# Two 64-row remainders of neighbouring batches put through the second feed-forward product as one block of 128 rows

## The chip, the cores and the metric

The kernel runs on one core of a Trainium2 chip. The metric is the time of one execution on the device in microseconds (us). The engines are TensorE (PE in the profile; PEld are its weight loads), VectorE (DVE), ScalarE (ACT), GpSimd (POOL) and SyncE (SP), which issues all transfers here.

## The reference

Eight batches of 576 tokens go through two parts. The first is attention with eight heads of 64 channels, in which each row of the scores keeps its 32 largest entries:

```python
scores = scale * np.matmul(q, k.transpose(0, 1, 3, 2))
kth = np.partition(scores, -top_k, axis=-1)[..., -top_k:-top_k + 1]
scores = np.where(scores >= kth, scores, -1000000000.0)
attn = softmax(scores); attn_out = np.matmul(attn, v)
```

The second is a feed-forward part on x (576 x 512 for a batch), with a convolution of three taps along the tokens as its gate:

```python
h = np.maximum(x @ w_in, 0.0)                        # 576 x 1024
conv_out = sum(conv_w[k] * hp[:, k:k + S, :] for k in range(3))
return (h * sigmoid(conv_out)) @ w_out               # 576 x 512
```

## The kernel before

Attention is cut into 288 tiles of 128 query rows: 8 batches x 4 pairs of heads x 9 tiles. `iteration(it)` writes one step of a pipeline in which each of five or six tiles is at another stage: PE makes the scores of tile it+3, ACT copies those of tile it+2 out of PSUM, DVE searches the candidates of tiles it and it-1 (L235, L255, L257), ACT and POOL mark and flip the entries of tile it-2 (L268, L273), ACT takes the exponential of tile it-3 (L280), DVE selects the threshold (`select`, L287) and weighs the exponentials of tile it-4 (L293), and PE transposes those of tile it-5 (L306) and multiplies them with v (L337, L340). Up to the last tile the order of the instructions on PE, ACT, DVE and POOL is that in which `iteration` writes them (a manual schedule). Behind it, in the tail, the framework's scheduler orders them.

The feed-forward part of a batch is laid between these steps. `ffn` (L567) cuts the 576 rows into part 0 (rows 0 to 255) and part 1 (rows 256 to 575). `Expand` (eight units for each part, one for each 128 columns of h) makes h with 12 matmuls (L404), relu on ACT (L418), the taps on POOL (in the tail on DVE, L457), tanh on ACT (L465) and the gate on DVE (L473); the result stays in the buffer `g0` or `g1`, of which each part has one. `Contract` makes the second product. Its `split` casts a piece of the gated h on ACT into a high part (L514), and POOL (DVE in the tail) subtracts to get the low part (L517). Then three matmuls for each 128 columns of h (high x high, high x low, low x high) add up in one PSUM bank, with the rows as the stationary operand and 512 columns of w_out as the moving one (L536). A block of 128 rows is two units of 12 matmuls (`half` 0 and 1, four of the eight column blocks each), since one slot of the `split` buffer holds 8 x 64 columns of high and of low part. The last 64 rows of a batch are one unit of 24 matmuls: eight column blocks with 64 rows each fill the same slot. `emit` copies the bank out (L552) and SP writes it to memory (L553).

A budget sets how much of this work an iteration gets: `run_units` spends a credit of 1.42 for each iteration (`FEED`), in units of planned cost, first on `Expand`, then on `Contract`. An `Expand` starts at most every second iteration (`PACE`), and not before every block of the same part of earlier batches has left `unready`, that is, has been read out of `g`. One `split` is written in an iteration, as long as fewer than three slots are taken (`SPB`). In the tail all of them are freer: four slots, several expands in flight, and both a PSUM bank of their own and one that the attention no longer needs (`mc`, `weights_ps`).

Of the kernel before, what the change touches and what calls it, by code (L numbers as in the profile page):

```python
# [63 lines left out]
def attend_and_feed(ctx: ExitStack, tc: tile.TileContext, q, k, v, weights, out, shared, finish=None):  # L64
# [313 lines left out]
    class Expand:  # L378
# [103 lines left out]
        def gated(self):  # L482
            self.gs["done"] = self.gs.get("done", 0) + 1
            state.flying -= 1

    class Contract:
        def __init__(self, b, part, s0, half, gs, box):
            self.b, self.part, self.s0, self.gs, self.box = b, part, s0, gs, box
            self.m = min(P, ROWS[part][1] - ROWS[part][0] - s0)
            nf = NFT * TAIL // self.m  # L490
            self.fs = range(half * nf, half * nf + nf)
            self.first, self.final, self.ready = half == 0, self.fs[-1] == NFT - 1, False
            self.count = nf
            self.cost = nf * 3 * (DM / 2400 + 0.012)

        def split(self):
            if not parts:
                parts.append(moe.tile([P, SPB, 2, NFT * TAIL], F32R, name="split"))
            late = state.it > NT + 4
            if late and len(parts) == 1:  # L500
                for pool, name, n, size in ((att, "e2", EBUFS, 2 * S), (att, "pT", 2, 2 * MAIN)):
                    for _ in range(n):
                        t = pool.tile([P, size], F32R, name=name, bufs=n)
                        extra.append(t[:, 0:2 * NFT * TAIL].rearrange("p (i c) -> p i c", i=2))
                parts.extend(extra)
            both = extra[state.split % len(extra)] if late else parts[0][:, state.split % SPB]
            self.hi, self.lo = (both[:, i].rearrange("p (f m) -> p f m", m=self.m) for i in range(2))
            self.late = late
            c0 = self.gs["at"] + self.s0
            src = self.gs["g"][:, self.fs[0]:self.fs[-1] + 1, c0:c0 + self.m]  # L510
            state.split += 1
            state.splits += 0 if late else 1
            state.late_splits += 1 if late else 0
            nc.scalar.copy(out=self.hi, in_=src)  # L514

            def rest(engine):
                engine.tensor_tensor(self.lo, src, f32(self.hi), ALU.subtract)  # L517
                self.ready = True
                unready.remove(self)

            if state.it > NT + 4:
                rest(nc.vector)
            else:
                pool_tasks.append((state.it + 1, 1.3, lambda: rest(nc.gpsimd)))
# [16 lines left out]
        def emit(self):  # L541
            m, mm = self.m, self.box.mm
            r = ROWS[self.part][0] + self.s0
            if state.it > NT + 4:
                if not outs_late:
                    t = const.tile([P, XBUFS * (S + 16)], F32, name="rows")
                    outs_late.extend(t[:, i * DM:(i + 1) * DM] for i in range(XBUFS * (S + 16) // DM))
                o = outs_late[0]
                outs_late.append(outs_late.pop(0))
            else:  # L550
                o = moe.tile([P, DM], F32, name="o", bufs=OB)
            nc.scalar.copy(out=o[0:m], in_=mm[0:m])  # L552
            nc.sync.dma_start(out=out[self.b, r:r + m, :], in_=o[0:m])  # L553

    parts, extra, outs_late, unready = [], [], [], []

    def split_next():
        if not unready or blocks or fetched or cut or acted or dved:
# [7 lines left out]
    def ffn(b, part):  # L566
# [2 lines left out]
        n = ROWS[part][1] - ROWS[part][0]  # L569
        for s0 in range(0, n, P):  # L570
            box = Box()
            units = [Contract(b, part, s0, half, gs, box) for half in range(1 if n - s0 == TAIL else 2)]
            contracts.extend(units)
            unready.extend(units)

# [365 lines left out]
```

## Time and profile before

| what | value |
|---|---|
| median of 3 runs | 1166.35 us (1164.91 to 1168.83) |
| profiled execution | 1168.88 us |
| its span (first to last instruction) | 1167.0 us |
| PE busy, PEld busy | 1056.8 us (91%), 775.1 us (66%) |
| DVE busy | 1066.8 us (91%) |
| ACT busy | 997.6 us (85%) |
| POOL busy | 896.1 us (77%) |
| matmuls of the second product (L536) | 960 |

The span has a beginning of some 200 us in which the weights are converted and no feed-forward work runs, a main part in which attention and feed-forward work share the engines, and from about 1076 us on the tail, in which only feed-forward work of the last two batches is left.

### The profile page before, as it was taken

The page shows a single profiled execution, that of the slowest core. Times are in us where ns is not written, and L with a number is a line of the kernel's source. Part 1 is how long each engine was busy: PE and PEld are TensorE (multiplying, and loading weights), DVE is VectorE, ACT ScalarE, POOL GpSimd, SP SyncE. Part 2 cuts the span into 40 slices and gives each one's busy share as a digit, 9 for nine tenths or more (in the row PEclk, how much of TensorE's full clock was granted, in tenths as well). Part 3 has the DMA queues.
Part 4 walks back from the last instruction along what each step waited for, and adds up shares of the span by engine and source line. Part 5 has one row for each costly group of instructions (what it writes and reads, how often), then busy time and mean ns, then how long its engine had stood idle before and what let it go on. Part 6 is the DMA issues. An engine that isn't in the chain of part 4 may idle for free.

```text
span 1167.0 us, 27441 instructions
## 1 busy us (share of the span) xinstructions
PE 1056.8 (91%) x8066; PEld 775.1 (66%) x8066; DVE 1066.8 (91%) x5832; ACT 997.6 (85%) x2335; POOL 896.1 (77%) x1072
## 2 busy tenths in 40 slices
PE   3665676888999999999999999999999999999996
PEld 1343344566767777776677777777777777777985
DVE  7999989999999999999999999999999999998550
ACT  5776778899999999999999999999999999998341
POOL 6778864789979888878879897888879887889100
PEclk9867659999999999999999999999999999999999
DMA  6220111101111111111111111111111111000001
GB/s 239 78 80 29 45 43 37 52 21 37 50 54 55 54 50 55 55 63 46 59 54 34 38 45 63 56 55 48 56 54 55 55 48 51 30 28 19 27 26 41
DMA packets 51695, 60.76 MB, mean 52 GB/s; under 512 B 9776, under 2 KB 30544, under 8 KB 51536
## 3 DMA queue, kind: packets, MB, share of 16 engines
q1 hardware_dynamic: 51536, 58.91, 15.8%
q8 instruction: 66, 1.08, 0.4%
q14 instruction: 93, 0.76, 0.2%
HBM read 49.31 MB, written 9.58 MB: 50 GB/s over the span
## 4 chain that ended last, share of the span: by engine, by line
PE 47%; DVE 42%; ACT 9%; issue 1%; DMA 0%; SPq 0%; POOL 0%; ACTq 0%; POOLq 0%
DVE cand L235 12%; PE mc L536 12%; DVE e L293 9%; PE me L404 8%; PE s_ps L337 6%; DVE z L283 6%; PE pt L306 6%; PE s_ps L219 5%; DVE cand L257 3%; DVE scratch L161 2%; ACT weights_ps L280 2%; PE s_ps L222 2%; DVE rows L255 2%; DVE hot L287 2%; PE weights_ps L536 2%; PE s_ps L214 2%
## 5 line engine op out<-in xcount | busy, mean ns | idle before, releaser
L273 POOL TENSOR_TENSOR z<-rows,side 128x579 f32<-128x579 f32 x288 | 347.9, 1208 | 148.6 <-ACT side L268 121.9
L235 DVE MAX8 cand<-rows 128x8 f32<-128x82 f32 (+1 forms) x2016 | 451.5, 238 | 0.1
L280 ACT ACTIVATE weights_ps<-rows,z 128x576 f32<-128x576 f32 x288 | 219.7, 763 | 41.4 <-DVE e L293 31.5
L293 DVE SCALAR_TENSOR_TENSOR e<-rows,kth,weights_ps 128x576 f32<-128x576 f32 x288 | 230.3, 800 | 0.3
L268 ACT ACTIVATE side<-rows 128x576 bf16<-128x576 f32 x288 | 223.9, 777 | 0.7 <-DVE rows L255 0.5
L404 PE MATMUL me<-x_hi,wi 128*128 128x322 f32 (+1 forms) x928 | 220.8, 310 | 1.2 <-ACT g L418 1.2
L228 ACT COPY rows<-s_ps 128x576 f32<-128x576 f32 x288 | 183.2, 636 | 38.8 <-PE s_ps L340 25.4
L283 DVE MAX8 z<-z 128x8 f32<-128x576 f32 x288 | 213.8, 742 | 0.0
L536 PE MATMUL mc<-wo,split 128*128 128x512 f32 (+1 forms) x756 | 205.1, 404 | 0.0
L219 PE MATMUL s_ps<-k,q 64*128 64x512 f32 x512 | 154.3, 680 | 51.2 <-ACT xt L348 36.7
L306 PE MATMUL pt<-ident,e 128*128 128x128 f32 x1152 | 191.7, 291 | 9.0 <-DVE e L293 9.0
L337 PE MATMUL s_ps<-pT,vn 128*64 128x128 f32 (+1 forms) x2560 | 171.2, 279 | 17.1 <-ACT rows L228 16.9
L337 PEld LDWEIGHTS s_ps<-pT,vn 128*64 128x64 f32 x2560 | 134.3, 143 | 54.0 <-ACT rows L228 25.7
L404 PEld LDWEIGHTS me<-x_hi,wi 128*128 128x128 f32 x928 | 157.5, 189 | 2.3 <-ACT g L418 1.9
L306 PEld LDWEIGHTS pt<-ident,e 128*128 128x128 f32 x1152 | 135.3, 148 | 35.3 <-issue 19.6
L311 ACT COPY pT<-pt 128x512 f32<-128x512 f32 x256 | 151.8, 593 | 3.8 <-PE pt L306 3.5
L536 PEld LDWEIGHTS mc<-wo,split 128*128 128x128 f32 (+1 forms) x756 | 126.5, 179 | 26.5 <-ACT o L552 0.2
L404 PE MATMUL me<-x_lo,wi 128*128 128x258 f32 (+1 forms) x464 | 138.8, 299 | 0.0
L437 POOL TENSOR_SCALAR t<-g,cr 128x256 f32<-128x256 f32 (+1 forms) x222 | 113.5, 511 | 0.0
L222 PEld LDWEIGHTS s_ps<-k,q 128*128 128x128 f32 x256 | 40.9, 201 | 104.9 <-issue 104.9
L255 DVE MAX8 rows<-cand 128x8 f32<-128x21 f32 x576 | 109.1, 189 | 0.0
L219 PEld LDWEIGHTS s_ps<-k,q 64*128 64x128 f32 x512 | 40.4, 193 | 83.8 <-ACT xt L348 47.5
(120 smaller groups left out, 1872.4 us busy)
## 6 DMA issues: line engine op xcount, KB each, us to landing
k<-in_k_dram SPq DMA_DIRECT2D x32, 352.0 KB
q<-in_q_dram SPq DMA_DIRECT2D x32, 288.0 KB
vn<-in_v_main_dram SPq DMA_DIRECT2D x32, 256.0 KB
rb<-row SPq DMA_DIRECT2D x64, 128.0 KB
out_dram<-o SPq DMA_DIRECT2D x24, 256.0 KB
raw<-in_w_in_dram SPq DMA_DIRECT2D x16, 256.0 KB
raw<-in_w_out_dram SPq DMA_DIRECT2D x16, 256.0 KB
vt<-in_v_tail_dram SPq DMA_DIRECT2D x32, 64.0 KB
```

Of the source, the lines that this page charges most:

```text
L219: nc.tensor.matmul(s_ps[:, 2 * h * BANK:(2 * h + 1) * BANK], lhsT=qx[d, at], rhs=kx[d, h * TAIL:h * TAIL + MAIN], start=True, stop=True)
L228: nc.scalar.copy(out=x, in_=s_ps[:, at:at + S])
L235: yield lambda c=c, at=at, n=n: nc.vector.max(out=t.cand[:, c:8 * CHUNKS:CHUNKS], in_=t.x[:, at:at + n])
L268: nc.scalar.activation(out=t.side[:, 2:S + 2], in_=t.x, func=AF.Sign, scale=-OVER, bias=t.row[:, 7:8], accum_out=t.cnt)
L273: nc.gpsimd.tensor_tensor(t.z[:, 8:S + 11], t.row[:, 6:S + 9], t.side, ALU.mult)
L280: nc.scalar.activation(out=e_ps, in_=t.x, func=AF.Exp, scale=scale, bias=t.shift)
L283: nc.vector.max(out=t.z[:, 0:8], in_=t.z[:, 10:S + 10])
L293: nc.vector.scalar_tensor_tensor(out=t.e, in0=t.x, scalar=kth[:, t.n:t.n + 1], in1=e_ps, op0=ALU.is_ge, op1=ALU.mult, accum_out=t.pc.sums[ ...
L306: nc.tensor.transpose(tp[:, i * P:(i + 1) * P], t.e[:, o + i * P:o + (i + 1) * P], ident)
L337: nc.tensor.matmul(a[r, 0:w], lhsT=st.pc.vn[:, h, i], rhs=st.pT[:, h if st.i < NI else 1 - h, i, 0:w], start=(i == 0), stop=False)
L404: nc.tensor.matmul(mm[:, 0:w], lhsT=wt, rhs=xx, start=(n == 0), stop=(n == len(ops) - 1))
L536: nc.tensor.matmul(mm[0:m], lhsT=x[:, i], rhs=wo[:, e, f], start=start, stop=stop)
```

## The change

The last 64 rows of an even batch are no longer a unit of their own. A `Keep` stands in their place in `unready`; its `split` copies the 8 x 64 gated columns into a buffer `ends` on ACT, and that is all. In the odd batch that follows, the last 64 rows become a block of 128 rows in two units like any other: rows 0 to 63 of the block are the kept ones, rows 64 to 127 its own. Each of its units casts and subtracts in two pieces of four times 64 columns, and its result goes out in two transfers, one for each batch. The number of feed-forward matmuls of the second product in the built program falls from 960 to 864; up to PE's last transposes they are 729 and 657. The first products are 1332 up to there in both.

```diff
+    class Keep:
+        def split(self):
+            c0 = self.gs["at"] + self.s0
+            kept = ends[self.b + 1] = moe.tile([P, NFT, TAIL], F32, name="ends")
+            nc.scalar.copy(out=kept, in_=self.gs["g"][:, :, c0:c0 + TAIL])
+            unready.remove(self)
+
     class Contract:
+        m = P
+
         def __init__(self, b, part, s0, half, gs, box):
-            self.m = min(P, ROWS[part][1] - ROWS[part][0] - s0)
+            self.two = ROWS[part][1] - ROWS[part][0] - s0 == TAIL
...
-            src = self.gs["g"][:, self.fs[0]:self.fs[-1] + 1, c0:c0 + self.m]
+            fs = slice(self.fs[0], self.fs[-1] + 1)
+            if self.two:
+                srcs = [(0, TAIL, ends[self.b][:, fs]), (TAIL, P, self.gs["g"][:, fs, c0:c0 + TAIL])]
+            else:
+                srcs = [(0, P, self.gs["g"][:, fs, c0:c0 + P])]
...
-            nc.scalar.copy(out=self.hi, in_=src)
+            for a, z, src in srcs:
+                nc.scalar.copy(out=self.hi[:, :, a:z], in_=src)
             def rest(engine):
-                engine.tensor_tensor(self.lo, src, f32(self.hi), ALU.subtract)
+                for a, z, src in srcs:
+                    engine.tensor_tensor(self.lo[:, :, a:z], src, f32(self.hi[:, :, a:z]), ALU.subtract)
...
-            nc.sync.dma_start(out=out[self.b, r:r + m, :], in_=o[0:m])
+            if self.two:
+                for i in range(2):
+                    nc.sync.dma_start(out=out[self.b - 1 + i, r:r + TAIL, :], in_=o[i * TAIL:(i + 1) * TAIL])
+            else:
+                nc.sync.dma_start(out=out[self.b, r:r + m, :], in_=o[0:m])
...
         for s0 in range(0, n, P):
             box = Box()
-            units = [Contract(b, part, s0, half, gs, box) for half in range(1 if n - s0 == TAIL else 2)]
+            if n - s0 == TAIL and b % 2 == 0:
+                unready.append(Keep(b, part, s0, gs))
+                continue
+            units = [Contract(b, part, s0, half, gs, box) for half in range(2)]
```

The change moves instructions on PE. The first place is where the last 64 rows of the first batch stood, in the iterations whose transposes are the 96th to the 98th; `mc` is the bank of the second product, `me` that of the first. Before:

```order
L306 MATMUL pt<-ident,e_5342 128x128 x4
L536 MATMUL mc<-wo,split 64x512 x9
L319 MATMUL me<-ident,e_5342 128x128
L219 MATMUL s_ps<-k,q 128x512 x2
L222 MATMUL s_ps<-k,q 128x2x64
L306 MATMUL pt<-ident,e_5455 128x128 x4
L404 MATMUL me<-x_hi,wi 128x322
```

And in the changed kernel:

```order
L306 MATMUL pt<-ident,e_5342 128x128 x4
L319 MATMUL me<-ident,e_5342 128x128
L219 MATMUL s_ps<-k,q 128x512 x2
L222 MATMUL s_ps<-k,q 128x2x64
L306 MATMUL pt<-ident,e_5455 128x128 x4
L404 MATMUL me<-x_hi,wi 128x322
```

The nine matmuls of the narrow unit are gone, and nothing stands in their place: this iteration has no feed-forward matmul. There are eleven such iterations from here to the last transposes, and none before.

The second place is the end of PE's work, behind the last first product (L404); `pT` and `e` are attention buffers that serve as slots of the split rows there. Before:

```order
L404 MATMUL s_ps<-x_hi,wi 128x322
L536 MATMUL mc<-wo,e_16572 128x512 x12
L536 MATMUL weights_ps<-wo,e_16573 128x512 x12
L536 MATMUL weights_ps<-wo,pT 128x512 x12
L536 MATMUL mc<-wo,pT 128x512 x12
L536 MATMUL mc<-wo,e_16572 128x512 x12
L536 MATMUL weights_ps<-wo,e_16573 128x512 x12
L536 MATMUL weights_ps<-wo,pT 128x512 x12
L536 MATMUL mc<-wo,pT 64x512 x24
```

And in the changed kernel:

```order
L404 MATMUL s_ps<-x_hi,wi 128x322
L554 MATMUL mc<-wo,e_16504 128x512 x12
L554 MATMUL weights_ps<-wo,pT 128x512 x12
L554 MATMUL mc<-wo,e_16503 128x512 x12
L554 MATMUL weights_ps<-wo,pT 128x512 x2
L554 MATMUL mc<-wo,e_16504 128x512 x2
L554 MATMUL weights_ps<-wo,pT 128x512 x10
L554 MATMUL mc<-wo,e_16504 128x512 x10
L554 MATMUL weights_ps<-wo,pT 128x512 x24
```

Behind the last first product stood 108 matmuls, now 84. The first of them that need the last gated columns (the second halves of the blocks of part 1) come after 36 matmuls; before, after 48. The last 24 are the block of 128 rows made of two batches.

## Rows read from the trace of the kernel before

**Rows 1.** Page, busy time of each engine over the span.

```profile
PE 1056.8 (91%) x8066; PEld 775.1 (66%) x8066; DVE 1066.8 (91%) x5832; ACT 997.6 (85%) x2335; POOL 896.1 (77%) x1072
```

**Rows 2.** Windows: length, then busy PE, PEld, DVE, ACT, POOL, PEclk, DMA share, GB/s.

```profile
200.00:300.00 100.00, 86.14 (x756) 64.23 (x755) 98.16 (x578) 92.42 (x218) 80.17 (x96) 0.98 0.17 52
300.00:400.00 100.00, 98.32 (x798) 73.40 (x797) 98.14 (x572) 95.30 (x224) 86.06 (x102) 1.00 0.16 51
400.00:1050.00 650.00, 644.72 (x5137) 475.46 (x5136) 623.72 (x3616) 611.00 (x1426) 552.24 (x647) 1.00 0.16 49
1076.00:1158.00 82.00, 82.00 (x470) 68.88 (x469) 36.15 (x72) 30.04 (x64) 8.10 (x10) 1.00 0.09 32
```

**Rows 3.** Groups by shape, 400 to 1060 us; behind the second bar the idle time before.

```profile
L287 DVE SCALAR_TENSOR_TENSOR hot<-weights_ps,cnt,z 128x10 f32<-128x10 f32 x187 | 40.7, 218 | 26.0 <-ACT weights_ps L465 17.6 <-ACT weights_ps L280 7.2
```

**Rows 4.** Waits of ACT, 400 to 1060 us: total, times, longest.

```profile
ACT rows L228 <- PE s_ps L340: 15.7, 28, 1.2
```

**Rows 5.** Chain of waits, 400 to 1050 us, by line.

```profile
by line: PE mc L536 13.4%; DVE cand L235 10.0%; PE me L404 9.9%; PE s_ps L337 8.1%; PE pt L306 7.9%; DVE e L293 7.8%; PE s_ps L219 7.7%; DVE z L283 4.8%; PE s_ps L222 3.0%; ACT weights_ps L280 2.8%; DVE cand L257 2.5%; PE s_ps L214 2.5%; AC
```

**Rows 6.** Chain of waits at the end: start, us, what.

```profile
1131.60 1.77 PE s_ps L404 x12
1133.37 2.75 PE mc L536 x12
1136.12 5.48 PE weights_ps L536 x24
...
1152.54 5.54 PE mc L536 x24
...
1158.10 0.58 ACT rows L552
```

**Rows 7.** Groups by shape, whole span, second product in the main part.

```profile
L536 PE MATMUL mc<-wo,split 128*128 128x512 f32 x612 | 166.1, 405 | 0.0
...
L536 PE MATMUL mc<-wo,split 128*64 128x512 f32 x144 | 39.0, 401 | 0.0
```

**Rows 8.** Groups by shape, whole span: what the added work resembles.

```profile
L517 POOL TENSOR_TENSOR split<-g,split 128x512 fp32r<-128x512 f32 x57 | 67.6, 1187 | 0.0
...
L514 ACT CAST split<-g 128x512 fp32r<-128x512 f32 x57 | 35.9, 630 | 0.1
...
L446 POOL TENSOR_TENSOR t<-t,g 128x256 f32<-128x256 f32 x56 | 35.8, 639 | 4.7
...
L465 ACT ACTIVATE weights_ps<-t,cw 128x256 f32<-128x256 f32 x49 | 23.4, 478 | 1.4
...
L552 ACT COPY o<-mc 64x512 f32<-64x512 f32 x6 | 3.5, 577 | 0.0
```

**Rows 9.** Timeline behind the last first product, from 1135.5 us.

```profile
1135.71 0.49 DVE L473 SCALAR_TENSOR_TENSOR g<-t,g 128x320 f32<-128x320 f32 x1 [0.69 <-ACT t L465]
...
1136.15 0.59 ACT L552 COPY rows<-mc 128x512 f32<-128x512 f32 x1 [0.47 <-PE mc L536]
1136.64 0.63 ACT L514 CAST e<-g 128x512 fp32r<-128x512 f32 x1
1137.30 0.69 DVE L517 TENSOR_TENSOR e<-g,e 128x512 fp32r<-128x512 f32 x1 [1.09 <-ACT e L514]
```

**Rows 10.** Line 553: duration of an output issue in ns, least/median/most.

```profile
L553 SPq DMA_DIRECT2D out_dram<-rows x10: 332/333/496, 1082.3 to 1158.7; - x10
```

**Rows 11.** Windows before the main part (columns as in rows 2).

```profile
178.00:185.00 7.00, 4.27 (x38) 2.63 (x36) 7.00 (x42) 6.67 (x17) 5.62 (x6) 1.00 0.00 1
...
255.00:262.00 7.00, 7.00 (x68) 5.69 (x68) 6.42 (x34) 5.95 (x17) 3.84 (x6) 0.78 0.17 46
```

**Rows 12.** Timeline of PE, 246 to 259 us.

```profile
246.83 1.09 PE L337 MATMUL s_ps<-pT,vn 128*64 128x128 f32 x16 [0.78 <-ACT rows L228]
...
254.63 0.35 PE L357 MATMUL pt<-ident,rec 128*9 128x128 f32 x1 [2.42 <-ACT pT L313]
...
255.13 1.98 PE L337 MATMUL s_ps<-pT,vn 128*64 128x128 f32 x16
```

More of the change, by code (lines that the diff above doesn't have):

```diff
@@ L484, in gated, with __init__ @@
             state.flying -= 1
+    class Keep:
+        def __init__(self, b, part, s0, gs):
+            self.b, self.part, self.s0, self.gs = b, part, s0, gs
+        def split(self):
[3 more added lines that the diff above has]
+            unready.remove(self)
     class Contract:
+        m = P
         def __init__(self, b, part, s0, half, gs, box):
             self.b, self.part, self.s0, self.gs, self.box = b, part, s0, gs, box
-            self.m = min(P, ROWS[part][1] - ROWS[part][0] - s0)
+            self.two = ROWS[part][1] - ROWS[part][0] - s0 == TAIL
             nf = NFT * TAIL // self.m
@@ L552, in emit @@
             nc.scalar.copy(out=o[0:m], in_=mm[0:m])
-            nc.sync.dma_start(out=out[self.b, r:r + m, :], in_=o[0:m])
-    parts, extra, outs_late, unready = [], [], [], []
+            if self.two:
[3 more added lines that the diff above has]
+                nc.sync.dma_start(out=out[self.b, r:r + m, :], in_=o[0:m])
+    parts, extra, outs_late, unready, ends = [], [], [], [], {}
     def split_next():
```

## The prediction

> **What bounds the kernel now.** I began with the busy times of the whole span [rows 1]: TensorE (PE) and VectorE (DVE) both stand at 91%, ScalarE (ACT) at 85%. That is an average over stages, so the busy times by stretch came next [rows 2]. The reader is to see three stages there. From 200 to 300 us DVE is the full one (98.16 of 100) and PE has 14 us to spare. From 400 to 1050 us PE is busy for 644.7 of 650 us, DVE for 623.7, ACT for 611.0: PE leads, but DVE has only 26.3 us of idle time and ACT 39.0, so PE's lead over the next limit is thin. From 1076 to 1158 us PE is busy without a break (82.00 of 82.00), and DVE and ACT have more than half of the time free.
>
> Third, who makes DVE wait [rows 3]: from 400 to 1060 us its idle time stands almost wholly before one instruction, `select` (L287, 187 times in 660 us, so a tile takes 3.53 us): 26.0 us, and 24.8 of them end with a write of ACT. ACT in turn waits for PE's scores there, 15.7 us of its idle time before one kind of copy alone [rows 4]. Fourth, the chain of waits [rows 5]. From 400 to 1050 us its PE entries in the row add up to 52.5% (13.4 + 9.9 + 8.1 + 7.9 + 7.7 + 3.0 + 2.5), and the second feed-forward product (L536) is the largest single entry, 13.4%. So it is on the path, but for about half of the time DVE or ACT carries the path. In the tail [rows 6] the chain is PE alone, to the last matmul and one ACT copy; 24 matmuls of L536 take 5.48 us there, and four such pieces follow one another.
>
> **What is removed.** Before, the last 64 rows of a batch are a unit of their own with 24 matmuls, each with 64 stationary columns and 512 moving ones. The rows by shape [rows 7] show that the narrow ones are not cheaper: 401 ns against 405 ns. These means overlap one another (a matmul begins before the last has ended), so the price is taken from the chain: 5.48 / 24 = 0.228 us [rows 6]. Two such units become one of 128 rows, so every pair of batches loses 24 matmuls. The order of PE's instructions counts 960 before and 864 after; up to the last transposes 729 and 657, behind them 231 and 207. The products of the first weight matrix are as many as before on both sides of that place, so nothing was pushed into the tail. That makes 72 x 0.228 = 16.4 us of PE time in the main part (three pairs) and 24 x 0.228 = 5.5 us in the tail.
>
> The Trainium skill ("TensorE: Matmul & The Clock Gate", section "Wait — 56ns, not 53.3ns?") gives 215.7 ns from start to start for 512 columns at the full clock. By it the 96 matmuls would be worth 20.7 us instead of 21.9; the trace's 228 ns decides here.
>
> **What it is worth in the tail.** All 5.5 us, since PE is the path there and the order shows the same run of first products with 24 matmuls fewer behind the last of them. What could take its place is the wait for the last first product: its relu, taps, tanh and gate end 2.83 us behind it (1133.37 to 1136.20) [rows 6, 9]. ACT then has one output copy (0.59) and two casts (0.63 each) and DVE two subtractions (0.69 each), together 6.1 us, before the first unit that needs them is ready. Before, PE had 48 matmuls to run meanwhile; after, 36, which is 8.2 us. That still hides it, with 2.1 us to spare. The combined unit's casts and subtractions come behind that and have more matmuls in front of them. The end pays a little: two output transfers instead of one. One more issue is 0.33 us [rows 10], and the second transfer lands behind the first. I take 0.4 us. Tail: -5.1 us.
>
> **What it is worth in the main part.** Three bounds. Upper: PE's 16.4 us. DVE's idle time allows less: in 200 to 300 us, where PE is not the limit, DVE still idles 1.84 of 100 us [rows 2], which is 12.0 us of 650, so of its 26.3 us about 14.3 can go with PE's lateness. Lower: the chain runs through PE for 52.5%; if only that share of the removed work shortens it, 16.4 x 0.525 = 8.6 us. Below that lies zero, if the moments at which DVE waits are ACT's own pile-ups. Above the lower one speaks that a saving made while the chain runs through DVE need not be lost: PE is then less late when DVE would next have waited. Against the upper one speaks that the order takes the work out in lumps: of the iterations from the 96th on, eleven have no feed-forward matmul at all after, and none before, and in such an iteration PE has some 2.1 us of work (3.5 less the usual six matmuls, 6 x 0.228) against DVE's 3.4 (623.7 / 650 x 3.53). I take the middle of 8.6 and 14.3, 11.4 us.
>
> What is added costs a little of it. ACT, for each pair of batches: before, two casts of 128x512 (0.63 each) and two output copies (0.58 each), 2.42 us; after, the keeping copy (taken as a cast, 0.63), four casts of 4x64 columns and one output copy. A form of that size on ACT is the tanh of 128x256, 0.478 us; half of the cast's is 0.315 [rows 8]. So 2.47 to 3.12 us, 0.05 to 0.70 more for each pair, 0.2 to 2.1 us for three. ACT is the engine that DVE waits for, so I count 1 us of it in full. GpSimd (POOL): two subtractions of 1.19 become four, for which the nearest row is 0.64 [rows 8]: 0.2 us more for each pair, hidden by its 98 us of idle time in 650; without that cover 0.6 us. SyncE issues two output transfers for each pair, as before. No new wait stands in front of other work: the keeping copy takes the place in ACT's order at which the cast of the same rows stood, and it needs the same gates; it frees the rows' buffer sooner than before, since no subtraction has to follow. Main part: -11.4 + 1 = -10.4 us.
>
> Sum: -10.4 - 5.1 = -15.5 us. The profiled execution took 1168.88 us (span 1167.0 and 1.9 around it), so it would be 1153.4. It lies 2.5 us above the median of the runs, 1166.35; against that the forecast is 1150.9 us.
>
> **Rivals.** *All of it counts.* If PE's lateness is behind every wait of DVE beyond the 1.84%, the main part gives 14.3 and the whole 19.4: 1147 us. For it: DVE's waits all end with ACT's writes, and ACT waits for PE [rows 4]. Against it: the lumps, and that a chain which leaves PE for 47% of the stretch must give some of it back.
>
> *DVE and ACT take over at once.* They have 26.3 and 39.0 us of idle time in 650; with three engines so near to one another the removed work may be given back as waits for the next. Then the main part gives 0 to 4 us and the tail its 5.1: about 1159 us. For it: the waits of DVE end with ACT [rows 3], which is busy for 94% of the stretch by itself. Against it: 200 to 400 us, in which DVE is at 98%, show that this machine can run closer to DVE's limit than 96%.
>
> *The clock falls (the slower side).* PE's granted clock is 1.00 from 400 us to the end of the work [rows 2]. Earlier, after an idle stretch of 2.42 us, it fell: the window behind it has 0.78 [rows 11], and sixteen matmuls of L337 took 1.98 us where they had taken 1.09 [rows 12], which is the lower of the two levels (1.2 and 2.4 GHz). The eleven iterations without feed-forward work are places where PE may now idle. If the clock fell in one of them, its 2.1 us of work would take 4.2 against DVE's 3.4, and the next iteration's 3.5 would take 7.0: 4.3 us lost at a place. The forecast's gain of 15.5 and the 3.5 us beyond which it counts as slower are used up by 19.0, so it decides from the fifth place on; at six, 25.8 us lost, the time is about 1177 us. Against it: PE idles there some 1.3 us (3.4 - 2.1), in pieces, and from 178 to 185 us it was busy for only 4.27 of 7 us with a granted clock of 1.00 [rows 11].
>
> The Trainium skill ("TensorE: Matmul & The Clock Gate", section "Part 1: The HAM clock gate") says that the low clock is the default and that activity lifts it, which is a rule against taking work from PE in lumps. The trace agrees in kind, with that one fall behind 2.42 us of idle time; no row shows one behind 1.3 us.
>
> *The change doesn't do what it says* is excluded by the counts above; only its pacing could differ, and the first products keep theirs.
>
> **How the numbers follow.** Forecast, 1147.5 to 1155.5 us: 0.60. All of it counts: 0.17. DVE and ACT take over: 0.18. Clock or another loss of that kind: 0.05. The range from 1145.5 to 1159.5 leaves out the third rival's worse half and the slow side. About 0.3% (3.5 us) is what a measurement of this kernel can tell from no change. The tail alone passes that, so faster holds the first two and nearly all of the third: 0.90. Same: 0.06, the third with a main part that loses what the tail gains, or a few falls of the clock. Slower: 0.04.
>
> **What would show it.** In the tail PE is busy without a break, and the piece from the end of the last first product to the end shrinks by 5 us; a gap before the second halves of the units would refute the cover. From 400 us to the end of the main part the 187 iterations take 3.47 to 3.49 us each, PE's busy share falls to 98%, DVE's rises to 97 to 98%, and the 26.0 us before `select` shrink to about 16. If they stay at 26 while PE idles, the second rival holds. A granted clock below 1.00 between 400 us and the end would show the third. The forecast is wrong if the main part keeps its length, or if the time is above 1159.5 us.

## The result, and the profile after

The change made the kernel faster: 1153.37 us (median of 4 runs, 1152.99 to 1155.28) against 1167.13 us for the kernel before, run beside it (4 runs, 1164.91 to 1168.83). The ratio is 0.9879, with a 95% interval from 0.9854 to 0.9904. The forecast was 1150.9 us with a range from 1145.5 to 1159.5. The profiled execution after took 1155.28 us, its span 1153.4.

The busy times of the page, for [rows 1], and the windows, for [rows 2] and the second half of [rows 11], with the same columns:

```profile
PE 1035.3 (90%) x7970; PEld 767.3 (67%) x7970; DVE 1064.5 (92%) x5834; ACT 996.5 (86%) x2343; POOL 895.6 (78%) x1078
```

```profile
200.00:300.00 100.00, 86.11 (x759) 64.17 (x754) 98.18 (x577) 92.35 (x218) 79.90 (x96) 0.98 0.17 52
400.00:1050.00 650.00, 634.25 (x5118) 473.78 (x5118) 627.01 (x3645) 616.23 (x1448) 559.06 (x661) 1.00 0.16 49
1070.00:1145.00 75.00, 75.00 (x439) 66.13 (x440) 36.00 (x74) 30.21 (x66) 8.42 (x10) 1.00 0.09 34
...
255.00:262.00 7.00, 7.00 (x68) 5.59 (x67) 6.43 (x35) 5.94 (x17) 3.84 (x6) 0.77 0.15 44
```

The reader is to see that from 400 to 1050 us PE now has 15.8 us of idle time where it had 5.3, that DVE came up by 3.3 us and ACT by 5.2, and that the granted clock is 1.00 from 400 us to the end. The tail is still PE without a break.

To place the gain I cut the profiled executions at two events that both kernels have: the end of tile 96's `weigh` (the 97th L293) and the end of the last first product (L404). Up to the first, both are alike (400.04 and 400.16 us). Between them lies the main part; behind the second the tail. The windows of the main part, before and then after (columns as in [rows 2]):

```profile
400.04:1133.37 733.33, 726.29 (x5699) 545.27 (x5698) 677.17 (x3769) 656.88 (x1531) 584.86 (x684) 1.00 0.15 46
```

```profile
400.16:1126.53 726.37, 709.82 (x5628) 540.87 (x5629) 675.24 (x3769) 656.35 (x1538) 586.13 (x691) 1.00 0.15 47
```

| stretch | before | after | difference |
|---|---|---|---|
| main part | 733.33 us (400.04 to 1133.37) | 726.37 us (400.16 to 1126.53) | -6.96 |
| PE busy in it | 726.29 | 709.82 | -16.47 |
| PE idle in it | 7.04 | 16.55 | +9.51 |
| tail, to the last matmul | 24.7 | 19.2 | -5.5 |
| from the last ACT copy to the end | 8.3 | 7.1 | -1.2 |

PE lost the 16.4 us of work that the prediction counted (16.47), but 9.5 of them came back as idle time of PE. Where that idle time stands, by the waits (400 to 1060 us: total, times, longest), for [rows 4], and by the group of `select`, for [rows 3]:

```profile
ACT rows L228 <- PE s_ps L340: 11.2, 21, 1.2
...
PE s_ps L219 <- ACT xt L348: 9.2, 11, 1.4
...
PE s_ps L214 <- ACT xt L348: 4.6, 6, 1.9
```

```profile
L287 DVE SCALAR_TENSOR_TENSOR hot<-weights_ps,cnt,z 128x10 f32<-128x10 f32 x189 | 40.7, 215 | 22.5 <-ACT weights_ps L465 16.4 <-ACT weights_ps L280 5.3
```

DVE's waits at `select` shrank only from 26.0 to 22.5 us. New are PE's own: before it writes scores (L219, L214) it waits 13.8 us for ACT to copy an attention block out of the PSUM tile `s_ps` (L348). The same rows of the kernel before hold 5.1 us:

```profile
PE s_ps L214 <- ACT xt L348: 4.3, 8, 0.9
...
PE s_ps L219 <- ACT xt L348: 0.8, 2, 0.6
```

The timeline of PE shows what stands around the larger of these waits (start, length, engine, line, what; in brackets the idle time before and its releaser):

```profile
399.36 0.27 PE L319 MATMUL me<-ident,e 128*128 128x128 f32 x1
400.77 1.13 PE L219 MATMUL s_ps<-k,q 64*128 64x512 f32 x4 [1.14 <-ACT xt L348]
...
663.05 0.66 PE L306 MATMUL pt<-ident,e 128*128 128x128 f32 x4
665.60 1.19 PE L214 MATMUL s_ps<-k,q 64*64 64x512 f32 x8 [1.89 <-ACT xt L348]
...
719.65 0.27 PE L319 MATMUL me<-ident,e 128*128 128x128 f32 x1
721.10 1.13 PE L219 MATMUL s_ps<-k,q 64*128 64x512 f32 x4 [1.18 <-ACT xt L348]
...
838.26 0.27 PE L319 MATMUL me<-ident,e 128*128 128x128 f32 x1
839.86 1.13 PE L219 MATMUL s_ps<-k,q 64*128 64x512 f32 x4 [1.32 <-ACT xt L348]
...
920.88 0.27 PE L319 MATMUL me<-ident,e 128*128 128x128 f32 x1
922.50 1.13 PE L219 MATMUL s_ps<-k,q 64*128 64x512 f32 x4 [1.35 <-ACT xt L348]
```

Between the transposes (L306, L319) and the scores (L219, L214) no feed-forward matmul stands. To count this over the whole timeline I cut it at the first transpose (L306) of each iteration, from the 96th on. Eleven iterations have no feed-forward matmul. They last 3.23 us in the mean and hold 12.1 us of PE's idle time, 1.1 us each; all the others together hold 4.7 us. Before, no iteration was without feed-forward matmuls, and all of them together held 7.0 us. These are the lumps of the prediction. What ACT does meanwhile, around the fourth of the waits shown:

```profile
836.04 0.59 ACT L311 COPY pT<-pt 128x512 f32<-128x512 f32 x1
836.52 0.76 ACT L280 ACTIVATE weights_ps<-rows,z 128x576 f32<-128x576 f32 x1
837.31 0.53 ACT L465 ACTIVATE weights_ps<-t,cw 128x320 f32<-128x320 f32 x1
837.78 0.76 ACT L268 ACTIVATE side<-rows 128x576 bf16<-128x576 f32 x1
838.45 0.19 ACT L268 ACTIVATION_READ_ACCUMULATOR side<-rows 128x1 f32 x1
838.54 0.62 ACT L228 COPY rows<-s_ps 128x576 f32<-128x576 f32 x1
839.06 0.58 ACT L311 COPY pT<-pt 128x512 f32<-128x512 f32 x1
839.53 0.27 ACT L348 COPY xt<-s_ps 128x128 f32<-128x128 f32 x1
```

ACT runs through all of it without waiting. In five windows that end with these five gaps, 18.29 us together, ACT is busy for 18.20, DVE for 16.79 and PE for 11.41. At these five places ACT's work fills the time, not PE's.

The chain of waits from 400 to 1050 us, by line, for [rows 5], and at the end, for [rows 6]:

```profile
by line: PE me L404 11.3%; PE mc L554 11.1%; DVE cand L235 9.9%; PE s_ps L219 7.9%; PE s_ps L337 7.9%; PE pt L306 7.6%; DVE e L293 7.6%; DVE z L283 5.1%; PE s_ps L222 3.1%; ACT weights_ps L280 2.9%; DVE cand L257 2.6%; PE s_ps L214 2.1%; AC
...
1124.76 1.77 PE s_ps L404 x12
1126.53 2.75 PE mc L554 x12
1129.28 2.73 PE weights_ps L554 x12
1132.01 2.75 PE mc L554 x12
1134.76 0.45 PE weights_ps L554 x2
1135.21 0.46 PE mc L554 x2
...
1140.25 5.46 PE weights_ps L554 x24
...
1145.74 0.58 ACT rows L570
```

The second product (L554, L536 before) fell from 13.4% to 11.1%. In the tail, 12 x 7 matmuls follow the last first product where 108 did, and no row of the chain shown is a wait.

### The profile page after: what moved, and what is told of

Same layout as the page of the kernel before. It is cut to its first block, busy times and chain, and to the rows that moved or that the text cites. A ratio compares the mean times of both kernels' runs of the same rounds, so it can differ in the third digit from the quotient of the medians.

```text
span 1153.4 us, 27267 instructions
## 1 busy us (share of the span) xinstructions
PE 1035.3 (90%) x7970; PEld 767.3 (67%) x7970; DVE 1064.5 (92%) x5834; ACT 996.5 (86%) x2343; POOL 895.6 (78%) x1078
## 4 chain that ended last, share of the span: by engine, by line
DVE 45%; PE 42%; ACT 11%; issue 1%; DMA 0%; SPq 0%; POOL 0%; ACTq 0%; POOLq 0%
DVE cand L235 13%; DVE e L293 9%; PE mc L554 9%; PE me L404 8%; DVE z L283 7%; PE s_ps L337 6%; PE s_ps L219 5%; PE pt L306 5%; DVE cand L257 3%; ACT weights_ps L280 2%; DVE scratch L161 2%; DVE rows L255 2%; PE s_ps L222 2%; DVE hot L287 2%; PE weights_ps L554 2%; PE s_ps L214 2%
## 5 line engine op out<-in xcount | busy, mean ns | idle before, releaser
L293 DVE SCALAR_TENSOR_TENSOR e<-rows,kth,weights_ps 128x576 f32<-128x576 f32 x288 | 230.1, 799 | 0.3
L404 PE MATMUL me<-x_hi,wi 128*128 128x322 f32 (+1 forms) x928 | 218.6, 308 | 1.2 <-ACT g L418 1.2
L219 PE MATMUL s_ps<-k,q 64*128 64x512 f32 x512 | 155.1, 684 | 59.6 <-ACT xt L348 44.9
L306 PE MATMUL pt<-ident,e 128*128 128x128 f32 x1152 | 191.8, 292 | 8.9 <-DVE e L293 8.9
L554 PE MATMUL mc<-wo,split 128*128 128x512 f32 x684 | 186.5, 406 | 0.0
L306 PEld LDWEIGHTS pt<-ident,e 128*128 128x128 f32 x1152 | 135.3, 148 | 35.3 <-issue 20.1
L404 PEld LDWEIGHTS me<-x_hi,wi 128*128 128x128 f32 x928 | 157.1, 189 | 2.4 <-ACT g L418 2.1
L404 PE MATMUL me<-x_lo,wi 128*128 128x258 f32 (+1 forms) x464 | 138.5, 299 | 0.0
L554 PEld LDWEIGHTS mc<-wo,split 128*128 128x128 f32 x684 | 120.1, 189 | 19.6 <-issue 0.2
L219 PEld LDWEIGHTS s_ps<-k,q 64*128 64x128 f32 x512 | 40.6, 194 | 91.2 <-ACT xt L348 58.8
```

Source lines behind the costliest of these rows:

```text
L219: nc.tensor.matmul(s_ps[:, 2 * h * BANK:(2 * h + 1) * BANK], lhsT=qx[d, at], rhs=kx[d, h * TAIL:h * TAIL + MAIN], start=True, stop=True)
L293: nc.vector.scalar_tensor_tensor(out=t.e, in0=t.x, scalar=kth[:, t.n:t.n + 1], in1=e_ps, op0=ALU.is_ge, op1=ALU.mult, accum_out=t.pc.sums[ ...
L306: nc.tensor.transpose(tp[:, i * P:(i + 1) * P], t.e[:, o + i * P:o + (i + 1) * P], ident)
L404: nc.tensor.matmul(mm[:, 0:w], lhsT=wt, rhs=xx, start=(n == 0), stop=(n == len(ops) - 1))
L554: nc.tensor.matmul(mm[0:m], lhsT=x[:, i], rhs=wo[:, e, f], start=start, stop=stop)
```

## The experiments

All were run beside the kernel before; ratios are to it. Its median was 1166.86 us in the first group (c0 to e3), 1167.01 in the second (e4 to e7), 1167.90 in the third. The time up to tile 96 varies by some 7 us from one execution to the next (last section), so each row also has the main part as cut above, which repeats: two executions of the changed kernel gave 726.37 and 726.35 us.

| run | median us (runs) | ratio, 95% interval | main part us | PE busy in it | PE idle in it |
|---|---|---|---|---|---|
| before | | | 733.33 | 726.29 | 7.04 |
| after | 1153.37 (4) | 0.9879 [0.9854, 0.9904] | 726.37 | 709.82 | 16.55 |
| c0_after | 1153.58 (6) | 0.9877 [0.9852, 0.9902] | 726.35 | 709.80 | 16.55 |
| e1 | 1157.69 (6) | 0.9914 [0.9886, 0.9942] | 729.03 | 711.11 | 17.92 |
| e2 | 1161.78 (12) | 0.9956 [0.9939, 0.9974] | 733.31 | 726.27 | 7.04 |
| e3 | 1154.77 (6) | 0.9895 [0.9863, 0.9926] | 724.83 | 711.85 | 12.98 |
| e4 | 1183.49 (4) | 1.0141 [1.0117, 1.0166] | 742.59 | 713.74 | 28.85 |
| e5 | 1185.36 (5) | 1.0149 [1.0129, 1.0169] | 741.55 | 729.08 | 12.47 |
| e6 | 1153.92 (4) | 0.9886 [0.9864, 0.9908] | 726.30 | 709.84 | 16.46 |
| e7 | 1180.35 (4) | 1.0113 [1.0089, 1.0136] | 739.96 | 714.51 | 25.45 |
| e8 | 1130.43 (4) | 0.9689 [0.9659, 0.9719] | 727.18 | 711.28 | 15.90 |
| e9 | 1141.53 (4) | 0.9790 [0.9756, 0.9823] | 732.37 | 725.78 | 6.59 |
| e10 | 1156.69 (9) | 0.9913 [0.9888, 0.9938] | 724.78 | 712.97 | 11.81 |
| e11 | 1143.90 (4) | 0.9802 [0.9770, 0.9834] | 713.16 | 687.41 | 25.75 |

**c0_after**, the changed kernel again, without an edit.

> The changed kernel again, as the control on the chip of the other three. Both theories: 0.986 to 0.990 of the kernel before. What lies behind the last output copy took 8.3 us before (1158.68 to 1166.99) and 7.1 us after (1146.32 to 1153.41) in one profile each; if that is chance, another profile shows 7 to 9 us.

It repeats the result. Its execution with a profile was 3.8 us longer than the one above, all of it before tile 96 (403.35 against 400.16 us).

**e1_half_narrow**, the kernel before with half of the narrow units' matmuls (half of the sum of these rows is left out): the same PE work taken out, and nothing added to ACT.

```diff
+            last = NFT // 2 - 1 if m == TAIL else NFT - 1
...
-                    start, stop = f + n == 0, f == NFT - 1 and n == 2
-                    nc.tensor.matmul(mm[0:m], lhsT=x[:, i], rhs=wo[:, e, f], start=start, stop=stop)
+                    start, stop = f + n == 0, f == last and n == 2
+                    if f <= last:
+                        nc.tensor.matmul(mm[0:m], lhsT=x[:, i], rhs=wo[:, e, f], start=start, stop=stop)
```

> The kernel before, in its own order; only the units of the last 64 rows run 12 of their 24 matmuls (half of the sum of these rows is left out). So PE loses the same 96 matmuls as in the change, in both batches of a pair, and ACT, POOL and SP work as before. Theory A (PE's saving is given back because ACT, and DVE through ACT, are the next limit): the same as the change within 2 us, about 1153 to 1155 us. Theory N (the change's own added work on ACT, the keeping copy and the split casts, eats the missing 9.5 us of the main part): the main part gains 10 us or more instead of 6.9, the time is about 1149 us. Theory L (the lumps): five iterations without feed-forward work instead of eleven, so 2 to 3 us better than the change, about 1151 us.

The median, 1157.69 us, is above what any of the three theories expected. The main part gave 4.3 us, less than the 7.0 of the change. So a gain as small as that, and smaller, comes about without the work added on ACT. Here too the matmuls go twelve at a time, and PE idles for 17.9 us. But theory L counted iterations without feed-forward work, and expected more from five of them than from eleven; it came out the other way. These five hold 4.1 us of the idle time. Where the rest comes from stays open.

**e2_tail_only**, the change for the last two batches alone.

```diff
+    def paired(b):
+        return b >= B - 2
...
-            if n - s0 == TAIL and b % 2 == 0:
+            if n - s0 == TAIL and b % 2 == 0 and paired(b):
...
```

> The change for the last pair of batches alone; the six batches before keep their units of 64 rows, so the main part stands in the order of before and the tail in that of the change. All theories: the tail gives 24 x 0.228 = 5.5 us, less 0.4 or more 1.2 us at the end: 1160 to 1162 us, ratio 0.994 to 0.996. If it gives less than 4 us, part of what I book to the tail comes from the main part's end.

The main part is that of before to 0.02 us, the tail that of after. The medians differ by 5.1 us (1166.86 - 1161.78), so the tail's term stands by itself.

**e3_feed34**, the changed kernel with `FEED` at 1.34.

```diff
-FEED = 1.42
+FEED = 1.34
```

> The changed kernel with a credit of 1.34 instead of 1.42 for an iteration, which spreads the feed-forward work: three iterations of the main part without a feed-forward matmul instead of eleven, and the same sums (3 matmuls of the second product move from the main part into the tail). Theory L: most of the missing 9.5 us of the main part is lost in those lumps, so this gains 3 us or more over the change, 1150 us or less. Theory A: it gains nothing, 1152 to 1155 us.

With three iterations without feed-forward work in place of eleven PE idles 3.6 us less, and the main part is 1.5 us shorter. The tail grew by 1.3 us, to 20.5: six matmuls of the second product more than after the change end behind the last first product (six of 0.228 us are 1.4). The medians show no gain, so theory L's 1150 us or less did not come. Some 1.5 us of the main part were lost to a fall of the clock in the profiled execution (next section, under the clock).

**e4_above_own**, the changed kernel with the constants that `select` compares with in SBUF, and **e5_before_above_own**, the kernel before with the same edit.

```diff
-    above, sums_ps = weights_ps[:, 2 * BANK - 32:2 * BANK - 22], weights_ps[:, 2 * BANK - 16:2 * BANK - 16 + NBLK]
+    sums_ps = weights_ps[:, 2 * BANK - 16:2 * BANK - 16 + NBLK]
+    above = const.tile([P, 10], F32, name="above")
```

> The changed kernel with the ten numbers that select compares with (`above`) in a tile of their own in SBUF; before, they lie in the PSUM tile weights_ps, into which ScalarE writes its exponentials (L280) and tanh (L465), and in the changed kernel's profile VectorE still waits at select (L287) for those two writes: 20.5 us between 400 and 1050 us, in 30 waits. Theory A (after the change ScalarE, and VectorE through it, is the next limit): select runs ahead of ScalarE's write, a wait of up to 0.7 us shrinks by the 0.6 us or so that select and what stands beside it take, 30 times; the stretch from tile 96's weigh to the end of the last first product, 726.4 us with the change, gets 3 to 8 us shorter, the time 1146 to 1150 us. Theory B (TensorE alone is the limit, with or without the change): the wait moves to the next VectorE instruction that needs the exponentials and the stretch stays within 1.5 us of 726.4; time 1152 to 1154 us.

> The kernel before with the same single edit (`above` in a tile of its own in SBUF), nothing else changed. Theory A (TensorE bounds before the change, the others only after it): the edit is worth less here than in the changed kernel, 0 to 2 us of the 733.3 us from tile 96's weigh to the last first product; time 1164 to 1167 us. Rival C (VectorE's waits at select cost the same with or without the change, so the two edits simply add): 3 to 8 us off, time 1159 to 1164 us. Theory B (TensorE alone in both): within 1 us of 733.3, as in the changed kernel.

All of these expectations failed: both kernels got slower, by 29.9 and 18.4 us (1183.49 - 1153.58, 1185.36 - 1167.01). The waits at `select` went, as meant, but the instruction itself took 408 ns in the mean in place of 215. The group in e4, 400 to 1060 us:

```profile
L288 DVE SCALAR_TENSOR_TENSOR hot<-above,cnt,z 128x10 f32<-128x10 f32 x185 | 75.4, 408 | 0.0
```

Behind the last bar stands no wait any more; the time is in the instruction. A piece of the timeline of e4 shows why:

```profile
399.75 1.42 POOL L373 TENSOR_TENSOR xt<-xt,rb 128x576 f32<-128x576 f32 x1
...
400.17 1.01 DVE L288 SCALAR_TENSOR_TENSOR hot<-above,cnt,z 128x10 f32<-128x10 f32 x1
```

DVE's instruction starts while one of POOL runs and ends with it: 400.17 + 1.01 = 401.18, 399.75 + 1.42 = 401.17. Of the 185 in this group, 104 took over 250 ns, and 103 of these end within 0.03 us of the end of a POOL instruction; the other 81 took the usual 0.2 us. With `above` in PSUM, 155 of 186 of them also start while POOL runs, and all take 199 to 230 ns. The Trainium skill ("SBUF — State Buffer", section "Who interferes with whom") says that a DVE instruction with two SBUF inputs contends with a GpSimd instruction that reads SBUF, and calls the ports that they share an exclusive lock. The trace agrees (103 of 104), and had I weighed that rule the expectation would have had the other sign.

The pair is of use all the same: with 0.19 us more of DVE's work in each tile DVE is the limit (645.07 and 646.56 of 650 us busy from 400 us on). There the change is worth nothing in the main part: 742.59 us with it, 741.55 without.

**e6_no_edge_copies**, the changed kernel without one of ACT's small copies (the two numbers beside each threshold are no longer recorded).

```diff
-            nc.scalar.copy(out=edge[:, t.n + 1 - n:t.n + 1], in_=rows[:, 0:n, 6:8])
+            pass
...
+    nc.gpsimd.memset(edge, 1.5)
```

> The changed kernel without ScalarE's copies of the two numbers beside the threshold into `edge` (L263: 26 copies, 5.5 us of ScalarE between 400 and 1040 us); the tile is set once at the start instead, so the test at the end that looks at them is left out in effect. TensorE's and VectorE's work in the main part stays as it is. Theory A (ScalarE's time counts now): the stretch from tile 96 to the last first product gets shorter by 2 to 5.5 us of 726.4; time 1148 to 1151.5 us. Theory B (TensorE alone): within 1.5 us; time 1152 to 1154 us.

Inconclusive. The main part stayed (726.30 us), as theory B had it, but ACT's busy time in it fell only by 1.56 us (656.35 to 654.79), because these copies overlapped their neighbours.

**e7_above_own_feed134**, e4 with `FEED` at 1.34.

> The changed kernel with `above` in a tile of its own in SBUF and FEED at 1.34 in place of 1.42, which spreads the second products more evenly over the iterations. By the profiles alone FEED 1.34 took 1.5 us more off the stretch from tile 96 to the last first product (724.8 us) and gave none of it in the medians. Theory A: both edits add, 4 to 9 us off the 726.4 us, time 1144 to 1149 us. Theory B: 1.5 us off at most, time 1151 to 1154 us.

It failed as e4 did, and for the same reason.

**e8_short_max_after** and **e9_short_max_before**: DVE relieved in both kernels; the search leaves out half of each row.

```diff
-        nc.vector.max(out=t.z[:, 0:8], in_=t.z[:, 10:S + 10])
+        nc.vector.max(out=t.z[:, 0:8], in_=t.z[:, 10:S // 2 + 10])
...
+        nc.vector.memset(kth, 1.5)
```

> The changed kernel with VectorE relieved: `below` (L283) looks for its maximum in the first half of the row only (288 of 576 columns; the other half of that search is left out, and the test at the end gets a constant), so one of VectorE's longest instructions, 742 ns for each tile, gets some 0.25 to 0.35 us shorter, 192 times behind tile 96. To be read with the same edit on the kernel before (the next run). Theory D (TensorE and VectorE stand so near each other that neither alone bounds; that is where the missing part of the gain went): with VectorE out of the way the change is worth nearly all of TensorE's 16.4 us, so the stretch from tile 96's weigh to the end of the last first product comes to 710 to 720 us here and the difference from the next run is 12 to 16.4 us (7.0 without the edit, -1.0 where select cost VectorE 0.19 us more for each tile). Rival E (ScalarE is what the freed time runs into): the difference stays at 5 to 9 us, and both get only a little shorter.

> The kernel before with the same relief of VectorE (half of `below`'s search left out, the test at the end gets a constant). Theory D: TensorE was already busy for 99% of the stretch, so it stays near it: 724 to 731 us in place of 733.3. If VectorE alone bounded the stretch it would shrink by 192 times 0.25 to 0.35 us, to 666 to 685 us. Rival E gives 724 to 731 as well, and is told apart by the run above.

Theory D failed here: it expected a difference of 12 to 16.4 us between the two main parts. The groups of e8 and then of e9, 400 to 1060 us:

```profile
L283 DVE MAX8 z<-z 128x8 f32<-128x288 f32 x183 | 81.1, 443 | 0.0
L287 DVE SCALAR_TENSOR_TENSOR hot<-weights_ps,cnt,z 128x10 f32<-128x10 f32 x184 | 41.0, 223 | 70.9 <-ACT weights_ps L465 44.5 <-ACT weights_ps L280 25.0
```

```profile
L283 DVE MAX8 z<-z 128x8 f32<-128x288 f32 x183 | 81.2, 444 | 0.0
L287 DVE SCALAR_TENSOR_TENSOR hot<-weights_ps,cnt,z 128x10 f32<-128x10 f32 x184 | 41.1, 223 | 75.2 <-ACT weights_ps L465 43.7 <-ACT weights_ps L280 30.6
```

The search takes 443 ns in place of 742, and all the time that DVE got back stands as a longer wait for ACT at `select`: 70.9 us where it was 22.5. The main part did not move (+0.8 us after, -1.0 before), and the change is worth 5.2 us in it (732.37 - 727.18), as rival E had it (5 to 9), though 732.37 us lies above the 724 to 731 that both theories gave for e9. Some 1.5 us of e8's main part are a fall of the clock (next section); without it the difference would be 6.7, an estimate. So DVE does not bound the main part of either kernel; it follows ACT, with whose writes its waits end. The whole time did fall, by 23.2 us against c0_after and by 26.4 us against the kernel before, and all of that lies before tile 96, which ends at 374.55 and 373.82 us: there DVE is the limit, as [rows 2] had it.

**e10_spread_cut** and **e11_third_cut**, the kernel before with 71 or 213 matmuls of the second product left out one by one in the main part.

```diff
             for i, f in enumerate(self.fs):
+                state.cuts = getattr(state, "cuts", 0) + (1 if f < NFT - 1 else 0)
+                drop = state.it <= NT + 4 and f < NFT - 1 and state.cuts % 3 == 0
...
-                    nc.tensor.matmul(mm[0:m], lhsT=x[:, i], rhs=wo[:, e, f], start=start, stop=stop)
+                    if not (drop and n == 2):
+                        nc.tensor.matmul(mm[0:m], lhsT=x[:, i], rhs=wo[:, e, f], start=start, stop=stop)
```

In e11 the condition on `cuts` is absent.

> The kernel before, order and pacing unchanged, with 71 of the 729 matmuls of the second product in the main part left out one by one, about every tenth (their part of the sums is missing); the change takes out 72 in lumps. The tail keeps all of its matmuls. TensorE's work falls by 71 x 0.228 = 16.2 us either way. Theory L (the lumps are why the main part gave 7.0 us and not 10.4): spread evenly the same work gives 10 to 14 us, the stretch comes to 719 to 723 us. Theory D (VectorE and ScalarE are the next limit at any place): 5.5 to 8.5 us, 725 to 728 us. The time is that stretch's gain less than the kernel before.

> As the run above, but with 213 of the 729 matmuls left out, every third one of all but the last three of a unit: 213 x 0.228 = 48.6 us of TensorE's work. Theory D: the stretch can't fall below what VectorE needs, which was idle for 27.8 us of tiles 90 to 282; the gain is 15 to 26 us (707 to 718 us), and VectorE is idle for some 5 to 10 us. If TensorE alone set the pace: 40 us or more. If ScalarE were the next limit already at the change's dose: less than 12 us.

The windows of the two main parts, e10 and then e11:

```profile
402.55:1127.33 724.78, 712.97 (x5636) 534.01 (x5635) 675.98 (x3769) 654.77 (x1531) 584.62 (x684) 1.00 0.15 47
```

```profile
396.01:1109.17 713.16, 687.41 (x5512) 511.92 (x5511) 674.01 (x3769) 652.30 (x1531) 583.72 (x684) 1.00 0.15 48
```

Taken out evenly, 13.3 us of PE's work in the main part (726.29 - 712.97) shortened it by 8.55 us, 0.64 for each microsecond; the change's lumps, 16.47 us, by 6.96, which is 0.42. By the matmuls missing in the windows it is 0.136 us for each of 63 (5699 - 5636) and 0.098 for each of 71 (5699 - 5628). e1 and e10 both leave out matmuls of the kernel before and add nothing: the twelves gave 4.3 us for 15.2 us of PE's work, the single ones 8.55 for 13.3. At three times the dose it is 20.2 of 38.9 us, 0.52.

The recorded ranges for e10 do not decide: 724.78 us stands between theory D's (725 to 728) and theory L's (719 to 723), since 63 of the 71 lay in the main part and not all. By the microsecond and by the matmul it speaks for the lumps. Scaled to the change, the two prices would make 10.6 us (0.64 x 16.47) or 9.6 (0.136 x 71): estimates. Even spread, part comes back: PE idles 11.81 us where it had 7.04. e11 has the size that theory D expected (713.16 us, in 707 to 718), and DVE's idle time from tile 90 to 282 is down from 27.8 to 11.5 us (5 to 10 expected): at that dose DVE is near its limit, which says nothing against e8 at the dose of the change.

## Why the prediction was right or wrong

**What is removed:** right. 16.4 us were counted for the main part, 16.47 measured as PE's busy time.

**The tail:** right. 5.5 us of matmuls predicted, 5.5 measured (24.7 to 19.2), and the cover held. Behind the last first product, for [rows 9]:

```profile
1128.87 0.49 DVE L473 SCALAR_TENSOR_TENSOR g<-t,g 128x320 f32<-128x320 f32 x1 [0.69 <-ACT t L465]
...
1131.06 0.69 DVE L535 TENSOR_TENSOR e<-g,e 128x512 fp32r<-128x512 f32 x1
...
1132.60 0.42 DVE L535 TENSOR_TENSOR pT<-g,pT 128x256 fp32r<-128x256 f32 x1
```

The gate ends 2.83 us behind the last first product, as before; the subtractions of the first units end at 1131.75 us, 3.0 us before the matmuls that need them (1134.76), where 2.1 were expected. The 0.4 us for a second output transfer did not show: the piece behind the last ACT copy is 6.9 to 8.6 us long over the fourteen profiled executions, a spread that hides it. The 1.2 us that the profile after gained there are within that spread too.

**The main part:** right in sign, too large in size: -10.4 us predicted, -7.0 measured. The step that failed is the middle between 8.6 and 14.3, in which the lumps have no price. Its upper end stood on DVE ("DVE's idle time allows less"), with an idle share taken from 200 to 300 us. e8 and e9 show that DVE's idle time there is no measure: give DVE 0.30 us less to do in each of 192 tiles, and it waits longer for ACT while the main part stays. Its lower end, the chain's share of 52.5%, came out nearer (8.6). What pulled the gain below even that are the lumps, which the prediction named and did not price: "in such an iteration PE has some 2.1 us of work". It had the price at hand: "PE idles there some 1.3 us", eleven times, is 14.3 us of idle time, and that stands in the rival of the clock, not in the sum. Measured are 12.1 us, in eleven iterations. I set PE's 2.1 us against DVE's 3.4; at the places shown it is ACT's back-to-back work that such an iteration waits for. Spread evenly, matmuls gave 0.64 of their time against 0.42, which for the change would have made 9.6 to 10.6 us (estimates of e10), near the 10.4 forecast; so most of the missing 3.4 us is put down to the lumps. Against a simple count of empty iterations stands e1, with fewer of them and a smaller gain. That the idle time of PE came back, and in which iterations, is measured; that ACT's order of work sets it is read from the waits and the timeline, since e6 changed ACT too little to test it.

The sum came out nearer than its terms. In the profiles the main part gave 3.4 us less than forecast and the tail with the end 1.6 us more (6.7 against 5.1), of which 1.2 is the spread at the end. To that extent the closeness is luck.

**The cost of the added work:** 1 us was taken of a range from 0.2 to 2.1. The groups after, 400 to 1060 us (columns: count, busy us, mean ns):

```profile
L535 POOL TENSOR_TENSOR split<-ends,split 128x256 fp32r<-128x256 f32 x6 | 4.4, 732 | 0.0
L535 POOL TENSOR_TENSOR split<-g,split 128x256 fp32r<-128x256 f32 x6 | 3.8, 640 | 0.0
L531 ACT CAST split<-g 128x256 fp32r<-128x256 f32 x6 | 2.5, 417 | 0.0
L531 ACT CAST split<-ends 128x256 fp32r<-128x256 f32 x6 | 2.5, 410 | 0.0
L493 ACT COPY ends<-g 128x512 f32<-128x512 f32 x2 | 1.3, 646 | 0.0
```

A cast of half the columns takes 0.41 us, between the 0.315 and the 0.478 of the prediction, and the keeping copy 0.646 (0.63). For a pair that makes 0.65 + 4 x 0.41 + 0.59 = 2.88 us, 0.46 more than the 2.42 of before. The size was right; e1, which adds none of it and gains less, speaks against its having decided.

**The clock:** right for the changed kernel: 1.00 from 400 us to the end of its work in both of its profiles. PE idles 1.89 us at the longest in the lumps, before the scores at 665.60 us, and the granted clock stays at its upper level (2.4 GHz) there. The earlier fall is where it was (0.77 from 255 to 262 us). But the rival is real. At the same place of e8 PE idled 1.80 us, and behind it, as in e3 behind 2.21 us, the clock fell to the lower level (1.2 GHz). e8, its scores, and then e3:

```profile
639.80:643.20 3.40, 3.40 (x30) 2.08 (x27) 2.43 (x15) 2.55 (x6) 3.23 (x5) 0.51 0.34 89
```

```profile
639.58 1.97 PE L214 MATMUL s_ps<-k,q 64*64 64x512 f32 x8 [1.80 <-ACT xt L348]
```

```profile
412.30:415.70 3.40, 3.40 (x33) 2.92 (x30) 2.98 (x15) 2.72 (x6) 3.32 (x5) 0.50 0.64 197
```

The scores took 1.97 us where they had taken 1.19. A fall cost some 1.5 us, not the 4.3 of the prediction: an estimate from the time between the end of the wait and the next first product, 3.81 us in e8 and 2.26 after. The length of the idle time alone does not decide, since 2.57 us in e4 (before 681.74 us) and 2.50 in e7 (before 424.50 us) left the clock at 1.00. An execution of the changed kernel could hold such a fall too; its two profiles show none.

**The rivals:** "DVE and ACT take over at once" is half true: the second half of its name holds at the places without feed-forward work that were looked at. "All of it counts" is excluded by PE's idle time. Of the signs named beforehand, an iteration takes 3.50 us (3.47 to 3.49 expected), PE is at 97.6% (98), DVE at 96.5 (97 to 98), `select` waits 22.5 us (about 16). All four lie on the side of the smaller gain.

**What stays open:** whether a different order of ACT's work in the iterations without feed-forward matmuls would give the 9.5 us back. PE's scores wait for a copy (L348) out of other columns of the same tile `s_ps`; a tile of its own for the attention blocks wasn't tried. Why e1 gained less than the change is open too. No variant that does the whole work beat the changed kernel in the medians.

## What to carry to other kernels

Work taken from the busiest engine counts only as far as the others let each iteration get shorter: before you price it, look whether it goes out evenly, because an iteration without any of it can be as long as the next engine's work (here 0.42 us of gain for each microsecond in lumps, 0.64 spread). An engine that is 96% busy and holds at least a quarter of the chain (9.9 + 7.6 + 5.1 + 2.6% for DVE) can still be a follower; ask whom its waits end with, and test by relieving it. Before an operand is moved to loosen a wait, ask what its place costs the instruction itself.

## What the runs showed of the hardware

- A DVE instruction of ten columns took 215 ns with one input in PSUM and 408 ns in the mean with both in SBUF, and 103 of the 104 longer ones in e4 ended with a POOL instruction (the longest took 1.38 us). The place of 10 numbers was worth 30 us of this kernel.
- The narrow form saves PE nothing: 401 ns for 64 stationary columns, 405 for 128 [rows 7], and after the change 24 full ones take 5.46 us where 24 narrow ones took 5.54 [rows 6].
- The time up to tile 96 varies between executions of one kernel (400.16 and 403.35 us for the changed one; 396.0 to 403.4 over all that leave DVE's work there as it was). In the longer ones the granted clock was 0.76 from 160 to 200 us and 0.91 to 0.92 from 200 to 240, in the shorter ones 0.84 to 0.96 and 0.96 to 1.00. With DVE's search halved it was 1.00 in both stretches, and the four runs of e8 lie within 1.4 us (those of e9 within 3.9).
